# Half blocks of the attention sums and key-value products on 128x64 array tiles, in a kernel of two linear and two sliding-window attention layers

## The chip, the cores and the metric

The kernel runs on one core of a Trainium2 chip. The engines named here are TensorE (PE, with its weight loads as PEld), VectorE (DVE), ScalarE (ACT), GpSimd (POOL) and the queue of SyncE (SP), which issues most transfers. The metric is the device time of one execution in microseconds (us).

## The reference, cut to what matters

Four attention layers of 32 heads, 16 wide, work on one sequence of 2048 tokens with 512 features. Layers one and three are linear attention (A), two and four sliding-window attention (B) with a window of 256 tokens. Each is added to the residual.

```python
def _A_ref(x, wqkv, wo):                       # layers 1 and 3
    q, k, v = ...                              # x @ wqkv, 32 heads of 16
    phi = lambda t: jnp.where(t > 0, t + 1, jnp.exp(t)) + 1e-6
    pq, pk = phi(q), phi(k)
    kv = jnp.einsum("bhsd,bhse->bhde", pk, v)  # summed over all tokens
    z = jnp.einsum("bhsd->bhd", pk)
    num = jnp.einsum("bhqd,bhde->bhqe", pq, kv)
    den = jnp.einsum("bhqd,bhd->bhq", pq, z)[..., None] + 1e-6
    return (num / den) ... @ wo

def _B_ref(x, wqkv, wo):                       # layers 2 and 4
    scores = jnp.einsum("bhqd,bhkd->bhqk", q, k) * (Dh ** -0.5)
    mask = (idx[:, None] - idx[None, :] >= 0) & (idx[:, None] - idx[None, :] < 256)
    p = _softmax(jnp.where(mask, scores, -1e9), axis=-1)
    return jnp.einsum("bhqk,bhkd->bhqd", p, v) ... @ wo

x = A_x
x = x + _A_ref(_layernorm(x), A_wqkv, A_wo)
x = x + _B_ref(_layernorm(x), B_wqkv, B_wo)
x = x + _A_ref(_layernorm(x), A_wqkv, A_wo)
x = x + _B_ref(_layernorm(x), B_wqkv, B_wo)
```

## The kernel before

The tokens are 16 tiles of 128. A linear layer goes over them twice: `a_kv` makes the normalised tile, its transpose `xTa`, phi(k) (`pk`) and v with a column of ones (`vA`), and `kv_mm` (L917) adds each tile's key-value product; once all sixteen are in, `sums` (L1229, the operations fin0 and fin1) masks the result into `kvz`. Then `a_q` and `a_out` make phi(q), the products with `kvz` (L947, the "normalised products") and the output projection. In layer one the sums over all tiles stay in PSUM; in layer three they are gathered in groups and added to `kvacc` on VectorE (L1328).

In a sliding-window layer a token tile is a block of 128 queries that sees six half blocks of 64 keys. Four of them are seen by all 128 queries (the scores `pF`, L1065); the oldest is seen by the first 64 queries only and the newest by the last 64 only (the scores `pH`, L1016). The scores run on row tiles of the array: 32 rows by 128 columns, four heads at a time. ScalarE takes the exponentials (L1086 for pF, L1044 for pH), VectorE multiplies the triangular masks in (L1104, L1052), and TensorE sums the weighted values: L1122 for the half blocks, L1134 for the full ones, into one bank `U` per two quarters of the heads (u0 and u1; the operations u0h and u1h are the half blocks). `vbd` holds the values laid out for two heads and their sum. A half block's matmul is a full 128x128 one. So that the 64 queries which don't see the block get zeros, `pH` has 192 columns per head: 64, then 64 that were set to zero once (`fill_pH`), then 64. The weight operand of the older block is columns 0 to 127, of the newer one columns 64 to 191. The first two token tiles have only the newer half block. The last tile of layer four has its own end, `b_end`, in four pieces (L1170 and L1179).

All operations of the four layers are recorded first, with what they read and write. A written list of numbers, `ORDER`, then gives the order: each word is an operation, a quote mark picks its second engine, and the figures behind a colon pick buffers or PSUM banks. `schedule` takes the words in turn, so each engine's program is the list's order cut down to that engine, and each engine works strictly in its own order. `emit` puts a semaphore wait only where an operation on another engine isn't known to have ended. PSUM has eight banks, and a score set takes two pairs of them. Sets such as `BYPE` say which transposes run on TensorE and not as a transfer, and the `"PE":` numbers beside an operation are the list maker's estimates of length.

A second program, `general`, is recorded beside it for inputs with values that are not finite; it isn't reached here.

Of the kernel before, what the change touches and what calls it, by code (L numbers as in the profile page):

```python
# [8 lines left out]
ACT = mybir.ActivationFunctionType  # L9
ALU = mybir.AluOpType  # L10
AP = bass.AP

P = 128
# [321 lines left out]
205:5.1 148 16 222' 23 272:1 273:13 192 214:6.7.0 215 163 244:7.0.3 245 184:3.1.2 177 216 218 302:2 285 185 286 246 174 303:14 248 250:4.2 251 229:2.2.1 230  # L335
265:7.3 287:3 247 217 249 186 178 266 188 26 219 259:6.3.3 260 274:3.4.0 233 252' 58 187 189 206 288:15 30 199:4.5.2 200 267 261 231 232 280:7.4 262 263 234
203 201 202 275 17 204 235:6.5 236 193 304:4.6.1 237' 207 20 31 264 276 278 277 279 32 33 305 306 307 308 309 289:5.1.2 281 290 208 291 292 293 294 295:6.6
# [6 lines left out]
617:4.3 618 619:0 448:2 405 851:0.2.0 415 852 853 416 631 592 632 417:3 625:7.2.5 406 633:0 626 878:4.0.1 622:6.3 623 648 879 880 649 467:3.10.3 468 627' 854  # L344
# [85 lines left out]
"""  # L430
PHIA = ("1.k","2.q","3.q")
HMD = ("2.a.", "3.a.")
BYPE = {("x1.", t) for t in range(4)} | {("a2.", 15), ("k2.", 15), ("o3.", 0), ("x3.", 0), ("a3.", 15)} | {("o2.",0),("x2.",0)}
VMOVE = {"POOL": 1.03}
KNEAR = {("3.b.", 0)}
LATE = 1
# [944 lines left out]
```

## Time and profile before

| what | us |
|---|---|
| median of three runs | 414.84 |
| lowest and highest | 413.82, 418.99 |
| the profiled execution | 414.87 |
| its span, first to last instruction | 413.6 |
| TensorE busy | 399.4 |
| ScalarE busy | 376.6 |
| VectorE busy | 370.5 |

The granted TensorE clock is 1.00 throughout. A busy share counts the time in which at least one instruction of the engine is under way; matmuls overlap each other, so for TensorE the step from one start to the next says more than the length of one. In the rows quoted later, "x16" counts instructions, `out<-in` names the tiles without their buffer numbers, and the last part tells what the engine waited for.

### The profile page before, as it was taken

How to read it: one execution, taken by the hardware profiler on the slowest of the kernel's cores; microseconds unless marked ns; L12 is line 12 of the kernel's file. 1: busy time of each engine (PE TensorE's matmuls, PEld its weight loads, DVE VectorE, ACT ScalarE, POOL GpSimd, SP SyncE). 2: the span in 40 equal slices, each digit the busy share in tenths (PEclk: the TensorE clock that was granted, in tenths of full speed). 3: DMA queues.
4: the chain of work that ended last, by engine and by line, in shares of the span. 5: the costliest groups of instructions: out<-in, count | busy, mean ns of one | idle time of the engine just before them, and what ended most of it. 6: DMA issues, size and time to landing. Idle time of an engine off the chain costs nothing.

```text
span 413.6 us, 18932 instructions
## 1 busy us (share of the span) xinstructions
PE 399.4 (97%) x8394; PEld 284.3 (69%) x8394; DVE 370.5 (90%) x979; ACT 376.6 (91%) x485; POOL 104.8 (25%) x204
## 2 busy tenths in 40 slices
PE   7999999999999999999999999999999999999998
PEld 2654877776676767777686678676767776867765
DVE  6996799999999999999998999999999999887873
ACT  5998769999999999999999467899999999999996
POOL 2420025162053121411313000260533232311300
DMA  8539224526243235222122102331375453261433
GB/s 259 145 84 217 43 61 80 101 60 99 46 55 57 48 51 69 50 35 61 42 49 55 41 2 40 70 75 32 80 81 76 68 107 34 55 93 30 58 54 92
DMA packets 76808, 29.48 MB, mean 71 GB/s; under 512 B 66352, under 2 KB 74672, under 8 KB 76720
## 3 DMA queue, kind: packets, MB, share of 16 engines
q1 hardware_dynamic: 71424, 22.63, 29.7%
q0 software_dynamic: 4096, 4.46, 6.1%
q8 instruction: 68, 1.11, 1.2%
q10 hardware_dynamic: 1200, 1.11, 0.9%
q14 instruction: 20, 0.16, 0.2%
HBM read 6.29 MB, written 2.10 MB: 20 GB/s over the span
## 4 chain that ended last, share of the span: by engine, by line
PE 50%; ACT 34%; DVE 11%; DMA 3%; issue 1%; SPq 0%; DVEq 0%
ACT pF L1086 24%; PE ps L863 21%; PE ps L875 10%; ACT pH L1044 7%; PE ps L1134 6%; PE ps L1065 5%; PE ps L1122 3%; DVE o L959 2%; DMA w_Av<-in_A_wqkv_dram 2%; PE ps L1016 1%; DVE stats L819 1%; DMA oT<-o 1%; PE ps L921 1%; PE ps L947 1%; DVE pk L890 1%
## 5 line engine op out<-in xcount | busy, mean ns | idle before, releaser
L1086 ACT ACTIVATE pF<-ps 128x1024 bf16<-128x1024 f32 x240 | 229.6, 1083 | 4.4 <-PE ps L1065 2.6
L822 POOL TENSOR_TENSOR rstd<-mv,const 128x1 f32<-128x1 f32 x64 | 37.6, 594 | 211.9 <-DVE mv L820 194.2
L990 POOL DMA_DIRECT2D vbd<-vt x128 | 67.3, 533 | 73.8 <-DVE vt L850 48.6
L1134 PE MATMUL ps<-vbd,pF 128*128 128x34 bf16 x1856 | 62.2, 178 | 1.9 <-issue 1.9
L1044 ACT ACTIVATE pH<-ps 128x1024 bf16<-128x1024 f32 (+1 forms) x64 | 60.3, 1014 | 2.6 <-PE ps L1016 2.3
L1134 PEld LDWEIGHTS ps<-vbd,pF 128*128 128x128 bf16 x1856 | 54.7, 96 | 8.4 <-issue 2.1
L1104 DVE TENSOR_TENSOR pF<-pF,const 128x512 bf16<-128x512 bf16 (+2 forms) x116 | 47.1, 413 | 5.6 <-ACT pF L1086 5.2
L1065 PE MATMUL ps<-qT,kbd 32*128 32x128 bf16 x1920 | 48.7, 217 | 1.9 <-ACT pF L1086 0.6
L884 ACT ACTIVATE E<-ps 128x512 bf16<-128x512 f32 x64 | 38.6, 622 | 10.4 <-PE ps L875 7.8
L819 DVE BATCH_NORM_STATS2 stats<-xres 128x6 f32<-128x512 bf16 x64 | 43.4, 684 | 1.9 <-DMA xres<-in_A_x_dram 1.6
L1052 DVE TENSOR_TENSOR pH<-pH,const 128x1024 bf16<-128x1024 bf16 (+1 forms) x64 | 41.1, 644 | 0.4 <-ACT pH L1044 0.4
L1065 PEld LDWEIGHTS ps<-qT,kbd 32*128 32x128 bf16 x1920 | 28.2, 92 | 17.7 <-ACT pF L1086 7.0
L875 PE MATMUL ps<-xT,w_Bk 128*128 128x128 bf16 x512 | 35.5, 219 | 0.7 <-ACT xT L850 0.3
L875 PE MATMUL ps<-xT,w_Bq 128*128 128x128 bf16 x512 | 35.6, 219 | 0.2 <-ACT pF L1086 0.2
L1122 PEld LDWEIGHTS ps<-vbd,pH 128*128 128x128 bf16 x928 | 29.2, 96 | 9.4 <-issue 3.1
L863 PE MATMUL ps<-w_Av,xTa 128*128 128x512 bf16 (+2 forms) x134 | 33.9, 369 | 1.4 <-DMA w_Av<-in_A_wqkv_dram 1.2
L875 PE MATMUL ps<-xTa,w_Aq 128*128 128x128 bf16 x512 | 34.8, 219 | 0.2 <-DVE pq L888 0.2
L863 PE MATMUL ps<-w_Bv,xT 128*128 128x512 bf16 (+2 forms) x144 | 34.2, 356 | 0.6 <-ACT pF L1086 0.3
L863 PE MATMUL ps<-w_Bo,oT 128*128 128x512 bf16 (+2 forms) x141 | 34.5, 354 | 0.3
L1122 PE MATMUL ps<-vbd,pH 128*128 128x34 bf16 x928 | 32.8, 178 | 1.3 <-DVE pF L1104 0.5
L863 PE MATMUL ps<-w_Ao,oT 128*128 128x512 bf16 (+2 forms) x145 | 33.7, 354 | 0.2
L863 PE MATMUL ps<-w_Ak,xTa 128*128 128x512 bf16 (+1 forms) x131 | 32.7, 374 | 0.6 <-ACT xTa L850 0.5
(98 smaller groups left out, 611.1 us busy)
## 6 DMA issues: line engine op xcount, KB each, us to landing
vbd<-vt POOLq DMA_DIRECT2D x128, 34.0 KB, 2.3
xres<-in_A_x_dram SPq DMA_DIRECT2D x16, 128.0 KB, 5.7
out_dram<-xres SPq DMA_DIRECT2D x15, 128.0 KB, 2.3
oT<-o SPq DMA_TRANSPOSE x60, 2.6
w_Ak<-in_A_wqkv_dram ACTq DMA_DIRECT2D x1, 512.0 KB, 5.5
w_Av<-in_A_wqkv_dram ACTq DMA_DIRECT2D x1, 512.0 KB, 7.6
w_Aq<-in_A_wqkv_dram SPq DMA_DIRECT2D x1, 512.0 KB, 6.6
w_Ao<-in_A_wo_dram SPq DMA_DIRECT2D x1, 512.0 KB, 5.8
```

The costliest lines, as they stand in the source:

```text
L819: s.op(n + ".st", {"DVE": 0.595}, lambda e, en: e.bn_stats(st0, x.h[:]), reads=[x], writes=[st])
L863: i = e.matmul(g.h[:, a:b], xT.h[:, kt, :], w.h[:, kt, a:b], start=(kt == 0), stop=(kt == 3), skip_group_check=True)
L875: i = e.matmul(g.h[:, f * P:(f + 1) * P], w.h[:, kt, f * P:(f + 1) * P], xT.h[:, kt, :], start=(f == 0 and kt == 0), stop=(kt == 3), skip_ ...
L884: s.op(n + ".e", {"ACT": _act_cost(512)}, lambda e, en: e.activation(E.h[:], g.h, ACT.Exp, bias=0.0), reads=[g], writes=[E])
L990: return [e.dma_start(vbd.h[64 * a:64 * a + 64, j, a], vt.h[64 * j:64 * j + 64, a]) for j in range(2)]
L1044: return e.activation(d, c, ACT.Exp, bias=0.0, scale=DH ** -0.5)
L1052: return e.tensor_tensor(v, v, tr, ALU.mult)
L1065: i = e.matmul(ss[r // 2].h[:, r % 2, k * P:k * P + P], kbds[fj[m] // 2].h[32 * r:32 * r + 32, f, fj[m] % 2, :], qT.h[32 * r:32 * r + 32, ...
L1086: s.op("e%d%d" % (u, g), {"ACT": _act_cost(1024)}, lambda e, en, S=ss[g], pb=pb, g=g: e.activation(pb.h[:, 2 * g:2 * g + 2, :], S.h, ACT.E ...
L1104: return e.tensor_tensor(v, v, tr, ALU.mult)
L1122: i = e.matmul(U.h[:, c:c + 34], pH.h[:, 4 * r + f, 64 * a:64 * a + P], vbds[j // 2].h[:, j % 2, :, 4 * f + r, :], start=first[0], stop=Tr ...
L1134: i = e.matmul(U.h[:, c:c + 34], pFs[at[f, m][0]].h[:, r, at[f, m][1] * P:at[f, m][1] * P + P], vbds[fj[m] // 2].h[:, fj[m] % 2, :, 4 * f ...
```

## The change

Every half block is now its own 64 queries wide. `pH` shrinks from 192 to 128 columns per head and needs no zeros. The matmul of the older half block uses the left 64 columns of the array and writes PSUM partitions 0 to 63, that of the newer one the right 64 columns and partitions 64 to 127; `tile_position` says so, and the two stand one behind the other. The key-value product of a quarter of the heads is cut in the same way: two matmuls with 64 columns of `pk` and 68 columns of `vA` where there was one of 128 by 136. Only a matching half of each former product was used, so the sums need one PSUM bank in place of two, `kvacc` half the size, and `sums` spreads them over the mask. In layer one the products are issued for four tiles at a time (`KV1`) and no longer tile by tile. The half-block sums no longer name the masked `pF` among what they read, and where there is no older half block they come behind the full blocks. One more of the first transposes is a transfer. `PHIP` is empty and changes nothing. `ORDER` is a new list.

```diff
 ORDER = """
-8 0 9 39 1 2 10 63:7 69 5 6 4 7 3 41 42 40 11 70 71 72 73:0 68 43 44 45 74:6.0 64 46 47 48 86 18 35 37 87 75 76:7.0.0 88 12 13 77 27 14 15 24 89:1 28 22
...
-BYPE = {("x1.", t) for t in range(4)} | {("a2.", 15), ("k2.", 15), ("o3.", 0), ("x3.", 0), ("a3.", 15)} | {("o2.",0),("x2.",0)}
+BYPE = {("x1.", t) for t in range(3)} | {("a2.", 15), ("k2.", 15), ("o3.", 0), ("x3.", 0), ("a3.", 15)} | {("o2.",0),("x2.",0)}
-LATE = 1
+KV1 = [4, 4, 4, 4]
+KV2 = [4, 4, 4, 2, 1, 1]
+PHIP = set()
...
-            self.r_pH = self.preset("pH", 3, [P, 16, 192], self.fill_pH())
+            self.r_pH = self.ring("pH", 3, [P, 16, P])
...
-    def kv_mm(self, pairs, dst, new, start):
+    def kv_mm(self, pairs, g, new, start):
         def mm(e, en):
-            d = dst()
             for n, (pk, vA) in enumerate(pairs):
                 for f in range(4):
-                    i = e.matmul(d[f // 2][:, (f % 2) * 136:(f % 2) * 136 + 136], pk.h[:, f * P:(f + 1) * P],
-                                 vA.h[:, 8 * f:8 * f + 8, :], start=(start and n == 0 and f % 2 == 0), stop=True,
-                                 skip_group_check=True)
+                    for c in range(2):
+                        i = e.matmul(g.h[64 * c:64 * c + 64, f * 68:f * 68 + 68], pk.h[:, f * P + 64 * c:f * P + 64 * c + 64],
+                                     vA.h[:, 8 * f + 4 * c:8 * f + 4 * c + 4, :], start=(start and n == 0 and f == 0), stop=True,
+                                     skip_group_check=True, tile_position=(0, 64 * c))
             return i
...
                         for a, j in pcs:
                             c = ((f % 2) * 4 + r) * 34
-                            i = e.matmul(U.h[:, c:c + 34], pH.h[:, 4 * r + f, 64 * a:64 * a + P], vbds[j // 2].h[:, j % 2, :, 4 * f + r, :],
-                                         start=first[0], stop=True, skip_group_check=True)
-                            first[0] = False
+                            i = e.matmul(U.h[64 * a:64 * a + 64, c:c + 34], pH.h[:, 4 * r + f, 64 * a:64 * a + 64], vbds[j // 2].h[:, j % 2, :, 4 * f + r, :],
+                                         start=(len(pcs) == 2 and f == 2 * g and r == 0), stop=True, skip_group_check=True, tile_position=(0, 64 * a))
...
-                        i = e.matmul(U.h[:, r * 34:r * 34 + 34], pH.h[:, 4 * r + f, 64 * a:64 * a + P], vbds[j // 2].h[:, j % 2, :, 4 * f + r, :],
-                                     start=(r == 0 and j == pcs[0][1]), stop=True, skip_group_check=True)
+                        i = e.matmul(U.h[64 * a:64 * a + 64, r * 34:r * 34 + 34], pH.h[:, 4 * r + f, 64 * a:64 * a + 64], vbds[j // 2].h[:, j % 2, :, 4 * f + r, :],
+                                     start=(r == 0), stop=True, skip_group_check=True, tile_position=(0, 64 * a))
...
-            self.kv_mm([(pk, vA)], lambda: (kvS.h[:, 0, :], kvS.h[:, 1, :]), [kvS] if t == 0 else [], t == 0)
+            group.append((pk, vA))
+            if len(group) == KV1[done]:
+                self.kv_mm(group, kvS, done == 0, done == 0)
+                group, done = [], done + 1
...
                 def acc(e, en, g2=g2, ngrp=ngrp):
-                    for hf in range(2):
-                        d = self.kvacc[:, 2 * hf:2 * hf + 2, :].rearrange("p f c -> p (f c)")
-                        i = e.tensor_copy(d, g2[hf].h[:, 0:272]) if ngrp == 0 else e.tensor_tensor(d, g2[hf].h[:, 0:272], d, ALU.add)
-                    return i
+                    d = self.kvacc[:].rearrange("p f c -> p (f c)")
+                    return e.tensor_copy(d, g2.h[:, 0:272]) if ngrp == 0 else e.tensor_tensor(d, g2.h[:, 0:272], d, ALU.add)
```

What the new list does to TensorE's order shows at three places. The first is the end of layer one's key-value phase; before, the products (L921) of single tiles follow the last value projections (`w_Av` with `xTa`), then a query projection (L875) and the first normalised products (L947):

```order
L863 MATMUL ps<-w_Av_135,xTa_63 128x512 x4
L863 MATMUL ps<-w_Av_135,xTa_62 128x512 x4
L921 MATMUL ps<-vA_122,pk_75 128x136 x4
L921 MATMUL ps<-vA_122,pk_70 128x136 x4
L921 MATMUL ps<-vA_122,pk_68 128x136 x4
L921 MATMUL ps<-vA_122,pk_71 128x136 x4
L921 MATMUL ps<-vA_122,pk_72 128x136 x4
L921 MATMUL ps<-vA_122,pk_69 128x136 x4
L921 MATMUL ps<-vA_122,pk_74 128x136 x4
L875 MATMUL ps<-xTa_53,w_Aq_136 128x128 x16
L947 MATMUL ps<-kvz_94,pq_77 128x136 x2
```

After, with L855 for the projections, L913 for the products, L867 and L935 for what follows:

```order
L855 MATMUL ps<-w_Av_137,xTa_63 128x448
L855 MATMUL ps<-w_Av_137,xTa_63 128x64
L913 MATMUL ps<-vA_122,pk_68 64x68 x8
L913 MATMUL ps<-vA_122,pk_70 64x68 x8
L913 MATMUL ps<-vA_122,pk_69 64x68 x8
L913 MATMUL ps<-vA_122,pk_73 64x68 x8
L913 MATMUL ps<-vA_122,pk_71 64x68 x8
L913 MATMUL ps<-vA_122,pk_74 64x68 x8
L913 MATMUL ps<-vA_122,pk_72 64x68 x8
L913 MATMUL ps<-vA_122,pk_75 64x68 x8
L867 MATMUL ps<-xTa_52,w_Aq_138 128x128 x16
L935 MATMUL ps<-kvz_94,pq_77 128x136 x2
```

The last two groups of four tiles stand together, and the last of them holds the tile whose value projection (`xTa_63`) comes just ahead.

The second place is in layer four, the half sums of one token tile between two score sets; before:

```order
L1065 MATMUL ps<-qT_100,kbd_125 128x128 x4
L1134 MATMUL ps<-vbd_132,pF_103 128x34 x16
L1122 MATMUL ps<-vbd_132,pH_133 128x34 x16
L875 MATMUL ps<-xT_46,w_Bk_138 128x128 x8
L1065 MATMUL ps<-qT_99,kbd_128 128x128 x4
```

After (L1052 scores, L1123 full-block sums, L1107 half-block sums):

```order
L1052 MATMUL ps<-qT_100,kbd_125 128x128 x4
L1123 MATMUL ps<-vbd_132,pF_103 128x34 x16
L1107 MATMUL ps<-vbd_132,pH_134 64x34 x16
L1123 MATMUL ps<-vbd_132,pF_107 128x34 x16
L1052 MATMUL ps<-qT_99,kbd_128 128x128 x4
```

The half sums keep their place among full-array matmuls, and are now of another tile shape than both neighbours.

The third place, a little later, shows half sums right behind a score set; before:

```order
L1065 MATMUL ps<-qT_101,kbd_126 128x128 x4
L863 MATMUL ps<-w_Bv_140,xT_45 128x512 x2
L1122 MATMUL ps<-vbd_132,pH_133 128x34 x16
L1134 MATMUL ps<-vbd_132,pF_107 128x34 x16
L1065 MATMUL ps<-qT_101,kbd_124 128x128 x4
```

After:

```order
L1052 MATMUL ps<-qT_101,kbd_126 128x128 x4
L1107 MATMUL ps<-vbd_132,pH_135 64x34 x16
L1123 MATMUL ps<-vbd_132,pF_105 128x34 x16
L1123 MATMUL ps<-vbd_132,pF_106 128x34 x16
L1052 MATMUL ps<-qT_98,kbd_125 128x128 x4
```

Here the three tile shapes follow each other: row tiles, column tiles, full array.

More of the change, by code (lines that the diff above doesn't have):

```diff
@@ L484, in run @@
             self.r_dn = self.ring("dn", 4, [P, 32], F32)
-            self.kvacc = self.tiles("kvacc", 1, [P, 4, 136], F32)[0]
+            self.kvacc = self.tiles("kvacc", 1, [P, 4, 68], F32)[0]
             self.r_vA = self.preset("vA", 8, [P, 32, 17], self.fill_vA())
@@ L1121, in pvH, with half, pvF @@
                             c = ((f % 2) * 4 + r) * 34
[L1122 to L1128 removed]
+                            i = e.matmul(U.h[64 * a:64 * a + 64, c:c + 34], pH.h[:, 4 * r + f, 64 * a:64 * a + 64], vbds[j // 2].h[:, j % 2, :, 4 * f + r, :],
+                                         start=(len(pcs) == 2 and f == 2 * g and r == 0), stop=True, skip_group_check=True, tile_position=(0, 64 * a))
+                return i
+            side = len(pcs) == 2
+            def half(new):
+                s.op("u%dh" % g, {"PE": 0.27 if side else 0.25}, pvH, reads=[pH] + [vbds[j // 2] for _, j in pcs], writes=[U], new=new, mode="c", kind="sum")
+            if side:
+                half([U])
             for f in (2 * g, 2 * g + 1):
[L1130 removed]
+                def pvF(e, en, f=f, g=g, U=U, side=side):
                     for r in range(4):
@@ L1134, in pvF @@
                             i = e.matmul(U.h[:, c:c + 34], pFs[at[f, m][0]].h[:, r, at[f, m][1] * P:at[f, m][1] * P + P], vbds[fj[m] // 2].h[:, fj[m] % 2, :, 4 * f + r, :],
-                                         start=False, stop=True, skip_group_check=True)
+                                         start=(not side and f == 2 * g and r == 0 and m == m0), stop=True, skip_group_check=True)
                     return i
-                s.op("u%d%d" % (g, f % 2), {"PE": 0.0252 * 4 * (4 - m0)}, pvF, reads=use(f) + [vbds[j // 2] for j in fj[m0:]], writes=[U], kind="sum")
+                s.op("u%d%d" % (g, f % 2), {"PE": 0.0252 * 4 * (4 - m0)}, pvF, reads=use(f) + [vbds[j // 2] for j in fj[m0:]], writes=[U],
+                     new=[U] if not side and f == 2 * g else [], kind="sum")
+            if not side:
+                half([])
             dn = self.r_dn.buf()
@@ L1306, in graph @@
         s.at = ("1.", base)
-        self.sums(lambda hf: kvS.h[:, hf, 0:272], kvz)
+        self.sums(lambda: kvS.h[:, 0:272], kvz)
         b1 = base + 0.1
@@ L1313, in graph @@
         ngrp = 0
-        groups = [4, 4, 4, 2, 1, 1]
+        groups = KV2
         for t in range(T):
@@ L1336, in graph @@
         s.at = ("2.", b2)
-        self.sums(lambda hf: self.kvacc[:, 2 * hf:2 * hf + 2, :].rearrange("p f c -> p (f c)"), kvz2)
+        self.sums(lambda: self.kvacc[:].rearrange("p f c -> p (f c)"), kvz2)
         self.segment("3.", b2, xTs2, kvz2, True)
```

192 lines of the change are left out of this document (89 added, 103 removed), and 75 rows, old and new, of the table ORDER.

## The prediction

> **What bounds the kernel now.** I read the page's busy shares first, then the busy time stage by stage, then what ScalarE waits for, then single stretches of TensorE's timeline.
>
> ```profile
> span 413.6 us, 18932 instructions
> PE 399.4 (97%) x8394; PEld 284.3 (69%) x8394; DVE 370.5 (90%) x979; ACT 376.6 (91%) x485; POOL 104.8 (25%) x204
> PE 50%; ACT 34%; DVE 11%; DMA 3%; issue 1%; SPq 0%; DVEq 0%
> ```
>
> Two engines are nearly full. The third line, the chain that ended last, is half TensorE and a third ScalarE. An average hides which of them binds where, so here is the same by stage. The first figure is the length, then the busy time of PE, PEld, DVE, ACT, POOL.
>
> ```profile
> 2.00:45.00 43.00, 41.30 (x296) 22.95 (x295) 33.83 (x113) 34.51 (x61) 9.05 (x16) 1.00 0.64 172
> 45.00:80.00 35.00, 34.01 (x590) 25.89 (x588) 34.08 (x95) 29.32 (x47) 8.67 (x16) 1.00 0.38 65
> 80.00:220.00 140.00, 137.18 (x3196) 99.07 (x3194) 130.70 (x332) 136.06 (x163) 38.97 (x72) 1.00 0.34 59
> 220.00:263.00 43.00, 42.19 (x655) 30.54 (x651) 40.11 (x111) 30.69 (x52) 5.70 (x11) 1.00 0.18 34
> 263.00:408.00 145.00, 140.19 (x3614) 103.24 (x3615) 128.58 (x322) 142.94 (x162) 41.61 (x78) 1.00 0.41 66
> 408.00:413.60 5.60, 3.70 (x57) 2.37 (x56) 2.25 (x8) 1.87 (x5) 0.00 (x0) 1.00 0.29 94
> ```
>
> From 2 to 80 us and from 220 to 263 us TensorE is full and ScalarE has gaps: 8.5, 5.7 and 12.3 us of them. From 263 to 408 us ScalarE is the full one: 142.94 of 145. What it waits for in that stretch (total, times, longest):
>
> ```profile
> ACT pF L1086 <- PE ps L1065: 0.8, 3, 0.5
> ACT pF L1086 <- PE ps L1072: 0.5, 1, 0.5
> ACT pH L1044 <- PE ps L1016: 0.2, 1, 0.2
> ```
>
> So 1.5 us at most of the last 145 us hang on TensorE. Between 80 and 220 us both are full.
>
> **What TensorE's work costs.** A "mode" is the tile shape of the array: full 128x128, or row tiles (32x128, the scores). The change adds column tiles (128x64). The trace holds no column tile, so its price has to come from neighbouring rows.
>
> ```profile
> 41.77 1.82 PE L921 MATMUL ps<-vA,pk 128*128 128x136 bf16 x28
> 43.42 1.06 PE L875 MATMUL ps<-xTa,w_Aq 128*128 128x128 bf16 x16
> 44.32 0.40 PE L947 MATMUL ps<-kvz,pq 128*128 128x136 bf16 x4
> ...
> 153.58 0.56 PE L1122 MATMUL ps<-vbd,pH 128*128 128x34 bf16 x16
> 154.08 0.40 PE L1065 MATMUL ps<-qT,kbd 32*128 32x128 bf16 x16
> 154.41 0.62 PE L875 MATMUL ps<-xT,w_Bq 128*128 128x128 bf16 x8
> ...
> 386.06 0.96 PE L1134 MATMUL ps<-vbd,pF 128*128 128x34 bf16 x32
> 387.14 0.41 PE L1016 MATMUL ps<-qT,kbd 32*128 32x64 bf16 x32
> 387.48 0.61 PE L863 MATMUL ps<-w_Bo,oT 128*128 128x512 bf16 x2
> ```
>
> The first figure is the start, the second the length. Matmuls overlap, so I take start to start.
> - Key-value products: (43.42 - 41.77) / 28 = 59 ns each, 0.236 us for the four of a token tile.
> - A 128-column full-array matmul: (44.32 - 43.42) / 16 = 56 ns.
> - Attention sums with 34 columns:
>
> ```profile
> L1134 PE MATMUL ps<-vbd,pF 128*128 128x34 bf16 x1856 | 62.2, 178 | 1.9 <-issue 1.9
> L1122 PE MATMUL ps<-vbd,pH 128*128 128x34 bf16 x928 | 32.8, 178 | 1.3 <-DVE pF L1104 0.5 <-ACT kt L850 0.2 <-ACT qT L850 0.2
> ```
>
> One lasts 178 ns; 32 in a row last 0.96 us, so the step is (0.96 - 0.178) / 31 = 25.2 ns, and sixteen cost 0.404 us.
> - A turn from one mode to another: sixteen sums ahead of row tiles take 154.08 - 153.58 = 0.50 us, 0.10 more than 0.404. The row-tile scores then take 0.33: four sets of four tiles stream 128 columns each, 4 x 56 = 0.224, so 0.106 is left for the turn back. I count **0.10 us a turn**.
> - A set of four row tiles with 64 columns: (387.48 - 387.14 - 0.10) / 8 = 30 ns.
>
> **The change, part by part.**
>
> *Half-block sums.* Of the 928 matmuls on L1122, 864 are 54 full groups of sixteen (27 token tiles, two groups each); 64 belong to the eight one-sided groups of the first two tiles of each layer. A full group becomes eight pairs. Bounds for a pair with 34 columns: 25 ns if it costs what one matmul costs now, 50 ns if nothing overlaps. I take **30 ns**, the row-tile set of 64 columns, the only row in which tiles share the array with so few columns. Per group 8 x 30 = 0.240 against 0.404: 54 x -0.164 = **-8.9 us** (range -11 to 0). One-sided groups have no partner: 8 x 8 x 5 ns = +0.3 us. The last tile's four groups of eight (L1170) go from 0.202 to 0.120: -0.3 us.
>
> *Key-value products.* Four matmuls become four pairs with 68 columns, between 30 ns (64) and 56 ns (128): 32 ns. 32 token tiles x (0.128 - 0.236) = **-3.5 us**.
>
> *Turns.* Counted over the whole order of TensorE, mode changes go from 306 to 381. 75 x 0.10 = **+7.5 us**. By stage: six more before the first normalised products, 28 up to the last key-value group of layer three, 36 to the last tile, five in the tail. The order shows why: a half group used to stand among other full-array sums, and is now an island between row tiles and full tiles, or between two full groups, which costs two.
>
> *Smaller edits.* Transposes on TensorE go from ten to nine: 4 x 56 ns = -0.2 us at the start. The tenth becomes a DMA on SP's queue, which sends the later tiles' transposes behind it; TensorE has the three tiles before it to work on meanwhile. The accumulation on VectorE halves:
>
> ```profile
> L1328 DVE TENSOR_TENSOR kvacc<-ps,kvacc 128x272 f32<-128x272 f32 x10 | 3.9, 433 | 0.0
> L705 ACT ACTIVATE pH<-const 128x1536 f32<-128x1536 f32 x1 | 1.5, 1506 | 0.0
> L850 ACT ACTIVATE qT<-ps 128x512 bf16<-128x512 f32 x12 | 7.6, 633 | 0.8 <-PE ps L875 0.8
> L850 DVE CAST qT<-ps 128x512 bf16<-128x512 f32 x20 | 13.7, 683 | 1.7 <-PE ps L875 1.6
> ```
>
> With its two copies it is twelve of about 0.43, now six: -2.6 us of VectorE, which TensorE hides between 180 and 247 us. The fill of pH goes (1.5 us of ScalarE at 14 us, in its slack), and ScalarE gives VectorE three 512-column copies on balance (0.63 each), all before the last stage. In that stage ScalarE's exponentials and copies stay the same in number, but for one of 128 columns at the very end. If VectorE's slack were gone, the three copies would cost 3 x 0.68 = 2 us. The half sums no longer wait for a masked pF; the L1122 row above shows 0.5 us of that wait, which I leave at nothing.
>
> *A new wait.* The last key-value group of the first phase needs four tiles at once, and stands right behind the last value projection. [...] After it the masking of the sums on VectorE (0.79 us in the first line below) is still covered by sixteen query matmuls (0.90):
>
> ```profile
> 43.63 0.79 DVE L1232 TENSOR_TENSOR kvz<-ps,const 128x272 bf16<-128x272 f32 x2 [1.96 <-PE ps L921]
> ```
>
> *Sum by stage*, on the path and off it:
> - To 44 us, TensorE bound: products -1.7, turns +0.6, transpose -0.2, wait +0.4: **-0.9**, all on the path.
> - 44 to about 250 us: 28 groups -4.6, four one-sided +0.2, products -1.7, turns +2.8: -3.3 of TensorE. ScalarE fills two thirds of this stretch as fully, so I carry half: **-1.7** (0 to -3.3).
> - The layer-four stage: 26 groups -4.3, one-sided +0.1, turns +3.6: -0.6, off the path, since ScalarE sets it: **0**.
> - Tail: sums -0.3, turns +0.5: **+0.2**.
>
> Together -2.4 us. The profiled execution took 414.87 us (span 413.6 and 1.3 around it), next to the median of 414.84, so I forecast **412.5 us**: within 2% (8.3 us), about what a measurement of this kernel can tell from no change.
>
> **The weight loads.** A load of 128 columns lasts 96 ns here, yet matmuls follow every 25 ns, so loads overlap each other about fourfold:
>
> ```profile
> L1122 PEld LDWEIGHTS ps<-vbd,pH 128*128 128x128 bf16 x928 | 29.2, 96 | 9.4 <-issue 3.1 <-DVE mv L820 0.4 <-DVE qT L850 0.4
> ```
>
> [...]
>
> **Rivals.**
> - *The halves do not overlap* (50 ns a pair, no gain in sums or products). Then only turns and the wait are left: +0.8 to 44 us, +2.8 after, up to +3.6 in the last stage, where TensorE has 4.8 us free, +0.5 in the tail: +4.1 to +7.7, about **420**. For it: 34 columns already step at 25 ns. Against: row tiles of 64 columns manage four in 30 ns.
> - *Each load is exposed*: half of 96 ns, one after the other. A full group costs 16 x 48 = 0.768, +0.364; the products of a tile 8 x 48 = 0.384, +0.148. To 44 us +3.2; then 28 x 0.364 + 2.4 + 2.8 = +15.4; last stage 9.5 + 3.6 less 4.8 free = +8.3; tail +1.2: **443**. Against: loads overlap in every mode that the trace has.
> - *Scores come late to the full ScalarE* (the slower side). TensorE works strictly in order, and an island of 0.24 and two turns, 0.44 us, now stands ahead of a score set in many places. If each of the 26 in the last stage shows as an idle gap of ScalarE, that is +11.4 from there: **424**. It decides once the islands use up the lead that TensorE has in PSUM, of eight banks four for a set. For it: 142.94 of 145 leaves nothing. Against: 1.5 us of such waits before, and TensorE's load is no higher than before.
> - *The new order packs better*: pairs at 25 ns (-1.0 to 44 us, -4.8 to 250 us, all on the path), and a quarter of ScalarE's 12.3 idle us between 220 and 263 filled, -3: **406**. One bank in place of two for the products speaks for it, nothing else.
>
> **How the numbers follow.** Forecast, with the case that nothing passes through, 410.5 to 415: 0.48. No overlap (419 to 422.5): 0.17. Scores late: 0.17. Better packed: 0.13. Loads exposed: 0.05. The 2% bounds are 406.5 and 423.1. Faster takes nearly all of "better packed", 0.12; slower takes the exposed loads and most of the late scores, 0.18; within 2% is 0.70. The range 405 to 421 leaves out the two slow cases' upper ends, 0.2.
>
> **What would show it.** In the profile after: the sixteen half sums start to start near 0.24 us beside other column work, and near 0.34 ahead of another mode; products 0.13 a tile; ScalarE still full in the last stage; the last stage as long as before; the first normalised products about 1 us earlier. The forecast is wrong if a pair costs over 50 ns, if a turn with column tiles costs far from 0.10, or if ScalarE's waits for scores grow past 5 us.

## The result

The changed kernel takes 411.86 us (median of 19 runs, 409.51 to 415.72) against 414.84 (19 runs of the kernel before). The ratio is 0.9928, with a 95% interval of 0.9902 to 0.9954: about 3 us faster, under 2% and clear of no change. The forecast was 412.5. Executions of one kernel differ in the mean granted TensorE clock (the kernel before, on one chip: medians of 414.3, 415.2 and 416.8 us at 1.00, 0.996 and 0.992), so differences near 1 us are also read from profiles at 1.00.

### The profile page after: what moved, and what is told of

Read it like the earlier page. It is cut to its first block, busy times and chain, and to the rows that moved or that the text cites. A ratio compares the mean times of both kernels' runs of the same rounds, so it can differ in the third digit from the quotient of the medians.

```text
span 410.6 us, 19193 instructions
## 1 busy us (share of the span) xinstructions
PE 395.3 (96%) x8539; PEld 277.5 (68%) x8539; DVE 370.6 (90%) x979; ACT 373.2 (91%) x481; POOL 107.4 (26%) x204
## 3 DMA queue, kind: packets, MB, share of 16 engines
q1 hardware_dynamic: 71968, 22.76, 29.5%
## 4 chain that ended last, share of the span: by engine, by line
ACT 45%; PE 30%; DVE 19%; DMA 3%; issue 1%; SPq 1%; POOL 0%; DVEq 0%; POOLq 0%
ACT pF L1073 34%; PE ps L855 11%; ACT pH L1031 8%; PE ps L867 7%; PE ps L1123 4%; DVE stats L811 3%; PE ps L1052 3%; DMA xres<-in_A_x_dram 2%; DVE o L947 2%; DMA xTa<-xn 2%; PE ps L1107 2%; PE ps L1004 1%; DVE xres L890 1%; DVE xn L817 1%; DVE E L877 1%
## 5 line engine op out<-in xcount | busy, mean ns | idle before, releaser
L814 POOL TENSOR_TENSOR rstd<-mv,const 128x1 f32<-128x1 f32 x64 | 39.5, 620 | 216.8 <-DVE mv L812 216.5
L1123 PE MATMUL ps<-vbd,pF 128*128 128x34 bf16 x1856 | 60.6, 178 | 0.3
L1123 PEld LDWEIGHTS ps<-vbd,pF 128*128 128x128 bf16 x1856 | 54.0, 96 | 7.5 <-issue 0.6
L1052 PE MATMUL ps<-qT,kbd 32*128 32x128 bf16 x1920 | 49.1, 217 | 2.9 <-ACT pF L1073 0.8
L1052 PEld LDWEIGHTS ps<-qT,kbd 32*128 32x128 bf16 x1920 | 28.5, 92 | 19.9 <-ACT pF L1073 8.0
L867 PE MATMUL ps<-xT,w_Bq 128*128 128x128 bf16 x512 | 36.2, 219 | 0.2
L867 PE MATMUL ps<-xT,w_Bk 128*128 128x128 bf16 x512 | 35.6, 219 | 0.4
L855 PE MATMUL ps<-w_Ao,oT 128*128 128x512 bf16 (+2 forms) x145 | 34.4, 355 | 0.9 <-ACT pF L1073 0.6
L855 PE MATMUL ps<-w_Ak,xTa 128*128 128x512 bf16 (+1 forms) x133 | 33.2, 371 | 1.9 <-DMA xTa<-xn 1.3
L855 PE MATMUL ps<-w_Bv,xT 128*128 128x512 bf16 (+2 forms) x148 | 35.1, 351 | 0.0
L855 PE MATMUL ps<-w_Bo,oT 128*128 128x512 bf16 (+2 forms) x149 | 34.3, 344 | 0.5 <-DVE mv L812 0.2
L867 PE MATMUL ps<-xTa,w_Aq 128*128 128x128 bf16 x512 | 33.9, 219 | 0.0
L855 PE MATMUL ps<-w_Av,xTa 128*128 128x512 bf16 (+2 forms) x141 | 32.6, 360 | 1.3 <-DMA w_Av<-in_A_wqkv_dram 1.3
L867 PEld LDWEIGHTS ps<-xTa,w_Aq 128*128 128x128 bf16 x512 | 29.9, 98 | 3.9 <-ACT pF L1073 0.7
L867 PEld LDWEIGHTS ps<-xT,w_Bq 128*128 128x128 bf16 x512 | 29.7, 98 | 4.1 <-issue 0.9
```

The source lines that it names most:

```text
L814: s.op(n + ".rs", {"POOL": 0.53}, lambda e, en: e.tensor_tensor(a_rs, v, self.half.h[:], ALU.pow), reads=[mv, self.half], writes=[rs])
L855: i = e.matmul(g.h[:, a:b], xT.h[:, kt, :], w.h[:, kt, a:b], start=(kt == 0), stop=(kt == 3), skip_group_check=True)
L867: i = e.matmul(g.h[:, f * P:(f + 1) * P], w.h[:, kt, f * P:(f + 1) * P], xT.h[:, kt, :], start=(f == 0 and kt == 0), stop=(kt == 3), skip_ ...
L1052: i = e.matmul(ss[r // 2].h[:, r % 2, k * P:k * P + P], kbds[fj[m] // 2].h[32 * r:32 * r + 32, f, fj[m] % 2, :], qT.h[32 * r:32 * r + 32, ...
L1123: i = e.matmul(U.h[:, c:c + 34], pFs[at[f, m][0]].h[:, r, at[f, m][1] * P:at[f, m][1] * P + P], vbds[fj[m] // 2].h[:, fj[m] % 2, :, 4 * f ...
```

## The profile after

The profiled execution took 411.86 us too. The page's first and fourth part:

```profile
span 410.6 us, 19193 instructions
PE 395.3 (96%) x8539; PEld 277.5 (68%) x8539; DVE 370.6 (90%) x979; ACT 373.2 (91%) x481; POOL 107.4 (26%) x204
ACT 45%; PE 30%; DVE 19%; DMA 3%; issue 1%; SPq 1%; POOL 0%; DVEq 0%; POOLq 0%
```

TensorE is busy 4.1 us less than before, VectorE the same, ScalarE 3.4 us less. In the chain that ended last ScalarE and TensorE have changed places. The same by stage (length, then PE, PEld, DVE, ACT, POOL):

```profile
2.00:45.00 43.00, 39.70 (x361) 21.17 (x360) 35.06 (x119) 31.10 (x59) 9.25 (x16) 1.00 0.76 188
45.00:80.00 35.00, 34.45 (x595) 26.29 (x592) 34.68 (x96) 29.32 (x45) 9.99 (x18) 1.00 0.39 67
80.00:220.00 140.00, 136.58 (x3287) 96.99 (x3285) 132.49 (x336) 136.34 (x162) 42.32 (x75) 1.00 0.32 55
220.00:263.00 43.00, 42.73 (x678) 31.00 (x677) 39.28 (x108) 32.86 (x55) 5.16 (x10) 1.00 0.21 36
263.00:408.00 145.00, 140.74 (x3626) 101.69 (x3623) 127.60 (x318) 141.91 (x162) 39.77 (x74) 1.00 0.38 66
```

In the first stage TensorE now idles 3.3 us, before 1.7. Between 220 and 263 us ScalarE works 2.2 us more than before in the same 43 us, so the work around it has moved together.

Fixed windows can't show where 3 us went, so the next cut is by events. The first row of each kernel goes from 80 us to the end of layer two's last exponential, the second from there to the start of layer four's first, the third to the end of layer four's last. Before:

```profile
80.00:228.96 148.96, 145.94 (x3385) 104.81 (x3383) 138.24 (x352) 144.88 (x174) 42.27 (x78) 1.00 0.33 57
228.96:261.65 32.69, 32.17 (x446) 24.27 (x443) 31.28 (x86) 20.52 (x39) 2.19 (x4) 1.00 0.16 30
261.65:408.87 147.22, 142.31 (x3653) 104.39 (x3652) 130.03 (x326) 145.16 (x165) 41.83 (x78) 1.00 0.41 67
```

After:

```profile
80.00:229.17 149.17, 145.75 (x3510) 104.00 (x3508) 140.11 (x356) 145.24 (x174) 42.88 (x76) 1.00 0.32 54
229.17:258.52 29.35, 29.08 (x384) 20.51 (x383) 27.25 (x77) 19.87 (x37) 2.19 (x4) 1.00 0.18 29
258.52:405.50 146.98, 142.72 (x3661) 103.58 (x3659) 130.82 (x326) 145.12 (x165) 42.17 (x78) 1.00 0.39 68
```

**The gain stands in one place.** Layer two ends where it did (229.17 against 228.96), layer four is as long as it was (146.98 against 147.22), and the stretch between them, in which TensorE is full and ScalarE a third empty, shrinks from 32.69 to 29.35 us. TensorE has 3.1 us less to do in it. Part of what is gone are query projections of layer three, which now stand ahead of layer two's end; before and after, in that stretch:

```profile
L875 PE MATMUL ps<-xTa,w_Aq 128*128 128x128 bf16 x176 | 11.9, 219 | 0.0
```

```profile
L867 PE MATMUL ps<-xTa,w_Aq 128*128 128x128 bf16 x144 | 9.4, 219 | 0.0
```

**What the new tiles cost.** TensorE's timeline in layer four and at the end of the first phase, after:

```profile
324.96 0.40 PE L1052 MATMUL ps<-qT,kbd 32*128 32x128 bf16 x16
325.29 0.43 PE L1107 MATMUL ps<-vbd,pH 128*64 128x34 bf16 x16
325.65 0.98 PE L1123 MATMUL ps<-vbd,pF 128*128 128x34 bf16 x32
...
41.80 0.70 PE L913 MATMUL ps<-vA,pk 128*64 128x68 bf16 x32
42.66 0.70 PE L913 MATMUL ps<-vA,pk 128*64 128x68 bf16 x32 [0.15 <-DVE vA L842]
43.29 1.07 PE L867 MATMUL ps<-xTa,w_Aq 128*128 128x128 bf16 x16
44.19 0.75 PE L935 MATMUL ps<-kvz,pq 128*128 128x136 bf16 x10
```

```profile
L1107 PE MATMUL ps<-vbd,pH 128*64 128x34 bf16 x928 | 25.1, 186 | 0.9 <-ACT vt L842 0.2 <-ACT kt L842 0.2 <-ACT pF L1073 0.2
L913 PE MATMUL ps<-vA,pk 128*64 128x68 bf16 x256 | 5.5, 196 | 0.2 <-DVE vA L842 0.2
```

Sixteen half sums are eight pairs: (0.43 - 0.186) / 7 = 35 ns a pair, 0.28 us a group. They take 0.36 us start to start ahead of full tiles, so the turn back is 0.08. The row tiles ahead of them take 0.33, as before, so the turn to column tiles costs the 0.10 that a turn cost then. Four token tiles of products: (0.70 - 0.196) / 15 = 34 ns a pair, 0.13 us a tile. The last key-value group shows an idle time of 0.15 us in its row; from start to start the 16 pairs ahead of it take 0.86 us (41.80 to 42.66) in place of 0.54, so the new wait costs TensorE 0.32.

**What came in unasked.** TensorE idles in the first phase for a transposed tile, and SP's queue shows why. TensorE and SP, after:

```profile
34.79 3.63 PE L855 MATMUL ps<-w_Ak,xTa 128*128 128x512 bf16 x16 [1.27 <-DMA xTa<-xn]
```

```profile
20.53 7.12 SPq L825 DMA_TRANSPOSE xTa<-xn  x5
27.69 0.58 SPq L771 DMA_DIRECT2D w_Ao<-in_A_wo_dram  x1
28.32 5.81 SPq L825 DMA_TRANSPOSE xTa<-xn  x3
```

Before, SP issued the load of `w_Ao` (512 KB) nearly last, with one transposition behind it; now three stand behind it:

```profile
19.12 12.33 SPq L833 DMA_TRANSPOSE xTa<-xn  x8
31.50 0.58 SPq L779 DMA_DIRECT2D w_Ao<-in_A_wo_dram  x1
32.12 1.19 SPq L833 DMA_TRANSPOSE xTa<-xn  x1
```

## The experiments

One profiled execution carries its own start: how long TensorE waits for the first weights differs from one to the next (1.2 us for `w_Av` before; 1.3 for `w_Av` and 0.6 for `w_Ak` after). So the table splits eight profiled executions, all at a mean granted clock of 1.00, at the start of the first normalised products.

| kernel | ratio to before [95%] | first normalised products, us | from there to the end of the span | layer two's last exponential to layer four's first | layer four's exponentials |
|---|---|---|---|---|---|
| before | 1 | 44.3 | 369.3 | 32.7 | 147.2 |
| changed | 0.9928 [0.9902, 0.9954] | 44.2 | 366.4 | 29.4 | 147.0 |
| sums on the full array | 0.9948 [0.9921, 0.9975] | 44.4 | 367.7 | 29.5 | 147.0 |
| products on the full array | 0.9909 [0.9877, 0.9941] | 42.9 | 367.2 | 29.7 | 147.2 |
| both on the full array | 0.9963 [0.9937, 0.9988] | 45.2 | 368.0 | 29.9 | 147.4 |
| old order, sums on column tiles | 1.0010 [0.9991, 1.0028] | 44.2 | 368.9 | 32.8 | 147.1 |
| halves in turn, not in pairs | 0.9971 [0.9947, 0.9994] | 42.9 | 367.9 | 29.6 | 147.3 |
| layer four's half sums twice | 1.0064 [1.0040, 1.0087] | 44.8 | 371.8 | 29.4 | 153.1 |

### Undoing the tiles, keeping the order

The half sums go back to 128 columns (`pH` is 192 wide again, with zeros in the middle, filled once):

```diff
-i = e.matmul(U.h[64 * a:64 * a + 64, c:c + 34], pH.h[:, 4 * r + f, 64 * a:64 * a + 64], vbds[j // 2].h[:, j % 2, :, 4 * f + r, :],
-             start=(len(pcs) == 2 and f == 2 * g and r == 0), stop=True, skip_group_check=True, tile_position=(0, 64 * a))
+i = e.matmul(U.h[:, c:c + 34], pH.h[:, 4 * r + f, 64 * a:64 * a + P], vbds[j // 2].h[:, j % 2, :, 4 * f + r, :],
+             start=(len(pcs) == 2 and f == 2 * g and r == 0 and a == 0), stop=True, skip_group_check=True)
```

> The changed kernel with its half-block sums (864 of 928 matmuls and the last tile's 32) back on the full array, in the same order of all engines; the products stay on column tiles, the result stays the reference's. In the changed kernel's trace a pair of half sums steps at 35 ns, so a group costs 0.28 us against 0.404: undoing adds 54 x 0.124 = +6.7 us of TensorE, and takes away 65 turns (381 to 316) x 0.095 = -6.2. Theory A (the sums nearly pay for their own turns; products and TensorE time freed ahead of layer four make the gain): 411.9 +- 1.2. Rival (the sums carry the gain): back to 414 or more. Rival (the new order carries the gain): 411.9 as well.

Measured: 413.69 us, 0.9948 [0.9921, 0.9975], 0.8 us above the changed kernel by the ratios and 1.3 us by the stretch behind the first normalised products. That lies between the theory's 411.9 and the rival's 414. The intervals overlap, so the size is open; both readings say that the turns saved pay for most of what the pairs bring, and that the pairs bring more.

The key-value products go back to four matmuls a tile:

```diff
-for c in range(2):
-    i = e.matmul(g.h[64 * c:64 * c + 64, f * 68:f * 68 + 68], pk.h[:, f * P + 64 * c:f * P + 64 * c + 64],
-                 vA.h[:, 8 * f + 4 * c:8 * f + 4 * c + 4, :], ..., tile_position=(0, 64 * c))
+i = e.matmul(g.h[:, f * 124:f * 124 + 136], pk.h[:, f * P:(f + 1) * P], vA.h[:, 8 * f:8 * f + 8, :], ...)
```

> The changed kernel with its key-value products on the full array again, four matmuls of 136 columns per token tile in place of eight of 68; sums stay on column tiles, same order. The four results overlap in the one bank, so the output is not the reference's; instruction count, sizes and waits are those of a full product. TensorE: 32 x (0.236 - 0.142) = +3.0 us, six turns fewer -0.6. All of it lies ahead of layer four. Theory A: +1.5 to +2.4 us, 413.4 to 414.3. Rival (order carries the gain): 411.9.

Measured: 411.55 us, 0.9909 [0.9877, 0.9941]. The theory that the products carry the gain falls: within the intervals nothing is lost without them. In the trace the wait for the transposed tile is gone instead. From 30 to 43 us, TensorE busy 11.57 us in the changed kernel and 12.95 here:

```profile
30.00:43.00 13.00, 11.57 (x133) 5.76 (x132) 9.16 (x29) 9.32 (x18) 0.00 (x0) 1.00 1.05 231
```

```profile
30.00:43.00 13.00, 12.95 (x110) 7.99 (x109) 9.43 (x32) 8.81 (x18) 0.00 (x0) 1.00 0.76 219
```

One reading is that the quicker products of the first phase only let TensorE reach a late tile sooner; but that wait differs between profiles of one order (more on it below), so it is not shown. Behind the first normalised products this kernel is 0.8 us longer than the changed one; the products of layer three, 16 x 0.10 us dearer here, would explain it.

Both edits together leave the new order with the smaller edits:

> Both undone, the new order alone: every matmul on the full array or on row tiles, 306 turns as before the change; output as with full products. TensorE: +6.7 + 3.0 - 7.1 = +2.6 us over the changed kernel. Theory A: 413.5 to 415, the time before the change. Rival (the new order carries the gain): 411.9 or less.

Measured: 414.35 us, 0.9963 [0.9937, 0.9988], near theory A. It is 1.5 us under the kernel before by the ratio, 1.3 us by the stretch behind the first normalised products, and 0.8 us where only executions at a granted clock of 1.00 are compared. Its cut by the same events as above:

```profile
80.00:231.06 151.06, 144.58 (x3457) 107.61 (x3491) 141.39 (x359) 146.36 (x175) 42.87 (x76) 1.00 0.33 54
231.06:260.91 29.85, 29.47 (x347) 21.27 (x351) 27.37 (x77) 19.86 (x37) 2.19 (x4) 1.00 0.18 29
```

The order shortens the stretch between the layers to 29.85 by itself. What it moves ahead of layer two's end then lengthens layer two: that ends at 231.06, 1.9 us later than in the changed kernel.

### The tiles in the old order

The kernel before, with its half sums on column tiles and nothing moved; the key-value products stay as they were:

```diff
-i = e.matmul(U.h[:, c:c + 34], pH.h[:, 4 * r + f, 64 * a:64 * a + P], ...)
+i = e.matmul(U.h[64 * a:64 * a + 64, c:c + 34], pH.h[:, 4 * r + f, 128 * a:128 * a + 64], ..., tile_position=(0, 64 * a))
```

> The kernel before with its two-sided half sums on column tiles, in its own old order; products, one-sided sums and everything else as before, the result stays the reference's. TensorE: 52 or 54 groups x -0.124 = -6.7 us, and mode changes go from 306 to 400, 94 x 0.095 = +8.9: +2.2 us. Theory (without the new order the turns eat the gain): 0 to +2 us over the time before. Rival (the tile shape gains in any order): -2 to -3.

Measured: 414.61 us, 1.0010 [0.9991, 1.0028], as expected. By the sum 400 turns against 306 eat what the pairs save, and the stretch between the layers stays at 32.8. Neither half of the change makes the 3 us: sums alone nothing, order alone about 1 to 1.5.

### Do the two halves overlap?

The sixteen matmuls of a group run left, left, ... right, right instead of left, right, left, right:

```diff
-for f in (2 * g, 2 * g + 1):
-    for r in range(4):
-        for a, j in pcs:
+for a, j in pcs:
+    for f in (2 * g, 2 * g + 1):
+        for r in range(4):
```

> The changed kernel with the sixteen half sums of a group in another order: all eight on the left 64 columns, then all eight on the right. Same instructions, tiles, waits and turns; neighbours no longer lie on different tiles. Theory (the 35 ns of a pair come from two tiles at work at the same time): each of the sixteen then takes about a pair's time, 31 to 35 ns, a group 0.50 to 0.56, +0.25 x 54 = +13 us of TensorE, about half of it in layer four where 4.3 are free: 418 to 422. Rival (a 64-column matmul simply costs 17.5 ns, paired or not): no change, 411.9.

Measured: 412.99 us, 0.9971 [0.9947, 0.9994]. The overlap is real: with the 186 ns of one from the second row, the group in the first row (layer four, the first ahead of a normalised product) steps at (0.58 - 0.186) / 15 = 26 ns a matmul, against 35 ns for two in a pair.

```profile
321.25 0.58 PE L1107 MATMUL ps<-vbd,pH 128*64 128x34 bf16 x16
...
L1107 PE MATMUL ps<-vbd,pH 128*64 128x34 bf16 x928 | 32.2, 186 | 0.7 <-ACT vt L842 0.2 <-ACT kt L842 0.2
```

A lone half sum is thus no dearer than a full-array one (25 ns), so a group costs 16 x 0.026 = 0.42 us in place of 0.28. That is 54 x 0.14 = 7.6 us of TensorE, of which 1.8 us showed by the ratios and 1.5 by the stretch behind the first normalised products: the size that was expected fell, the overlap did not.

### How much of TensorE's time passes through

The half sums of 28 groups ahead of layer three's key-value end (layer two) run twice, the second run starting the bank anew, so that the sums stay the same; then the same is done in layer four (`"3.a."`):

```diff
-def pvH(e, en, g=g, U=U):
-    for f in (2 * g, 2 * g + 1):
-        for r in range(4):
+def pvH(e, en, g=g, U=U, again=2 if len(pcs) == 2 and s.at[0] == "2.a." else 1):
+    for f, r in [(f, r) for _ in range(again) for f in (2 * g, 2 * g + 1) for r in range(4)]:
```

> The changed kernel with the 28 two-sided groups of half sums of layer two issued twice (the second pass writes the same bank anew, the result stays the reference's). That is 28 x 0.28 = +7.8 us of TensorE between 60 and 229 us. Theory (TensorE's work before layer four sets the time nearly one for one, since what it can't do there of layer three's projections is left for the stretch without exponentials): +5.5 to +8, 417.5 to 420. Prediction's half share: +3.9, 416. Rival (ScalarE, 136 of 140 us busy there, sets it): 0 to +2.

Measured: 418.30 us, 1.0088 [1.0056, 1.0120]. The busy time of the half sums (25.1 us in the changed kernel) is 32.0 here, so TensorE had 6.9 us more to do, and by the ratios the kernel became 6.6 us longer, give or take 1.7 by the intervals: layer two passes TensorE's time on nearly one for one.

> The same in layer four: 26 groups twice, +7.3 us of TensorE between 263 and 403 us, where ScalarE is busy 141.9 of 145 us and TensorE 140.7. Theory (ScalarE sets layer four, TensorE has some 4.3 us free): 0 to +3.5, 412 to 415.5. Rival (TensorE sets it as well): +7, 419.

Measured: 417.59 us, 1.0064 [1.0040, 1.0087], 5.6 us longer (give or take 1.4) for 6.7 us of extra work (half sums 31.8 us in place of 25.1); layer four's exponentials take 153.1 in place of 147.0. The share passed on is not told apart from layer two's. The theory that ScalarE alone sets layer four falls. ScalarE's groups from 258 us on, in the changed kernel and in this one:

```profile
L1073 ACT ACTIVATE pF<-ps 128x1024 bf16<-128x1024 f32 x120 | 114.0, 1126 | 0.9 <-PE ps L1052 0.7
L1031 ACT ACTIVATE pH<-ps 128x1024 bf16<-128x1024 f32 (+1 forms) x32 | 30.5, 1045 | 1.2 <-PE ps L1004 1.1
```

```profile
L1073 ACT ACTIVATE pF<-ps 128x1024 bf16<-128x1024 f32 x120 | 114.4, 1034 | 3.6 <-PE ps L1052 1.7 <-PE ps L1059 1.2
L1031 ACT ACTIVATE pH<-ps 128x1024 bf16<-128x1024 f32 (+1 forms) x32 | 29.3, 972 | 1.9 <-PE ps L1004 1.7
```

The idle time ahead of exponentials grows from 2.1 to 5.5 us. The mean of one full-block exponential falls (1126 to 1034 ns) while the busy time does not: 120 of them add up to 135.1 us in 114.0 us of busy time in the changed kernel and to 124.1 in 114.4 here, so the time in which two run at once falls from 21.1 to 9.7 us. A late score set costs the wait here, and the overlap with it. TensorE is busy 144.5 of those 153.1 us and is not full either, which points to the place of the longer sums in its order and not to their total.

### The late tile

In the changed kernel the load of `w_Ao` goes behind the three transposing transfers on SP's queue, one word of the list:

```diff
-183 231:0 232:12 57 197:3.0 136 166
+183 231:0 232:12 197:3.0 136 166
...
-254:6.3 205:5.2.1 223 289:15 58 59
+254:6.3 205:5.2.1 223 289:15 57 58 59
```

> The changed kernel with one word of the order moved: SP issues the load of the output weights of layer one behind the last three transposes of the first phase and no longer ahead of them. In the changed kernel TensorE stands 1.27 us at 33.5 us for such a transpose (xTa), three of which take 5.8 us there. Theory (the load of 512 KB delays the transposes): the wait goes, -0.5 to -1.2 us, 411. Rival (the transposes are late for another reason, their tiles or other loads): no change.

Measured: 410.29 us, 0.9872 [0.9829, 0.9915]. Both kernels once more, side by side on one chip:

> The changed kernel once more, as the mark for the three below on one chip. Expected: 411.9 us, 0.993 of the kernel before (0.990 to 0.996). It holds the 1.27 us stall of TensorE at 35 us, ahead of the key projection that waits for a transposed tile.

> The changed kernel with one transfer moved: the load of w_Ao stands one place later on SP's queue, behind the three transposing transfers instead of ahead of them. Theory (the stall at 35 us lies on the path and is carried to the end): about 1.3 us under the changed kernel on the same chip, 410.5, 0.990 of the kernel before. Rival (what is saved at 35 us is lost again at a later wait, layer two being held by ScalarE too): within 0.4 us of the changed kernel.

Measured: 411.91 us, 0.992 [0.989, 0.995], for the changed kernel and 410.67, 0.9897 [0.9866, 0.9928], with the later load: 1.24 us apart, with overlapping intervals and the same sign both times. At a granted clock of 1.00 each of the five executions with the later load (410.6 to 411.0) lies below each of the five without (411.1 to 412.9). SP's queue then, the stretch from 30 to 43 us, and TensorE's key projections to 44 us, which wait for weights only:

```profile
20.50 13.70 SPq L825 DMA_TRANSPOSE xTa<-xn  x8
34.25 0.58 SPq L771 DMA_DIRECT2D w_Ao<-in_A_wo_dram  x1
```

```profile
30.00:43.00 13.00, 12.85 (x159) 7.03 (x158) 10.00 (x34) 9.62 (x19) 0.00 (x0) 1.00 0.74 207
```

```profile
L855 PE MATMUL ps<-w_Ak,xTa 128*128 128x512 bf16 (+1 forms) x65 | 15.8, 376 | 0.5 <-DMA w_Ak<-in_A_wqkv_dram 0.5
```

SP is through with the last transposition no earlier (28.32 + 5.81 = 34.1 us in the changed kernel, 34.2 here), so it isn't SP's time that the tile missed. With the load ahead, its 512 KB move in the same stretch as the last transposing transfers: issued at 27.69 us, they land 5.0 us later. The transposing transfers of the changed kernel between 24 and 40 us take 3.0 us from issue to landing (the median of six), and 2.6 here; from 30 to 43 us the DMA share, the last but one figure of the row, is 1.05 in the changed kernel and 0.74 here. That the load's packets held the tile back is the reading that fits, and it is not shown: with products on the full array the load stands ahead too, and the share is 0.76 and there is no wait; with the halves in turn it is 1.05 and the wait 0.2 us. The wait is no constant either: in the nine profiles with the load ahead it is 0 to 1.8 us, in the three with it behind there is none. This is the fastest kernel of the case.

### Four copies to VectorE

Four copies out of PSUM in layer four get the quote mark that gives them to VectorE:

```diff
-1956:0 1982 2015 2010:0
+1956':0 1982' 2015' 2010':0
```

> The changed kernel with four copies out of PSUM of layer four given from ScalarE to VectorE, nothing else moved. ScalarE has 2.5 us less to do in layer four (4 x 0.63), VectorE about 2.7 us more of its 16 us of slack there, TensorE the same. Theory A (ScalarE alone sets the last stage): 2 to 2.5 us under the changed kernel, 409.5. Theory B (TensorE is as full there, as the doubled half sums of layer four let suppose, which cost 5.6 of their 7.0 us): 0 to 0.8 us under it, 411.5.

Measured: 417.50 us, 1.0058 [1.0031, 1.0085]: 5.6 us slower than the changed kernel on that chip, outside both theories. In the profile nearly all of it is one place. ScalarE and VectorE there:

```profile
324.60 5.61 ACT L1073 ACTIVATE pF<-ps 128x1024 bf16<-128x1024 f32 x6 [0.51 <-PE ps L1052]
334.26 1.02 ACT L1073 ACTIVATE pF<-ps 128x1024 bf16<-128x1024 f32 x1 [4.06 <-PE ps L1052]
```

```profile
329.32 0.69 DVE L842 CAST qT<-ps 128x512 bf16<-128x512 f32 x1 [1.24 <-PE ps L867]
331.84 0.69 DVE L842 CAST kt<-ps 128x512 bf16<-128x512 f32 x1 [1.06 <-PE ps L867]
332.90 0.69 DVE L947 TENSOR_TENSOR o<-ps,dn 128x512 bf16<-128x512 f32 x1
```

And TensorE:

```profile
330.74 1.07 PE L867 MATMUL ps<-xT,w_Bk 128*128 128x128 bf16 x16 [1.46 <-DVE o L1138]
331.64 0.40 PE L935 MATMUL ps<-kvz,pq 128*128 128x136 bf16 x4
333.73 0.49 PE L1052 MATMUL ps<-qT,kbd 32*128 32x128 bf16 x16 [1.69 <-DVE o L947]
```

VectorE's copy of `qT` waits for the query projection, and behind it on VectorE stands the division (L1138) that frees the bank TensorE needs for the key projection; the copy of `kt` then waits for that projection, and behind it stands the division (L947) that frees the bank of the next scores. Two waits each way, 4.06 us without a score for ScalarE. VectorE had 16 us to spare in the stage, and none in its order. The run is therefore no test of whether ScalarE sets the stage.

Right behind the two waits TensorE's granted clock falls, and ScalarE waits for scores once more:

```profile
334.00:337.00 3.00, 3.00 (x65) 1.54 (x53) 2.11 (x6) 1.94 (x2) 0.00 (x0) 0.50 0.23 49
337.19 1.94 ACT L1031 ACTIVATE pH<-ps 128x1024 bf16<-128x1024 f32 x2 [0.98 <-PE ps L1004]
```

The clock, the last but two figure of the first row, is 0.50 for some 3.3 us, and the wait behind it 0.98 us. All twelve executions have a mean clock of 0.988 to 0.996, five of the six of the changed kernel on that chip 1.00. So the 5.6 us hold the ring of waits and a slower clock. Whether the waits bring the clock down is not shown: behind the 1.27 us that TensorE stood idle in the changed kernel it stayed at 1.00.

> Both edits together: the later load of w_Ao and the four copies on VectorE. If both gains are real and apart, their sum: by theory A of the copies 408 us, by theory B 410, 0.984 to 0.989 of the kernel before. If the first gain is lost again later, as much as the copies alone give.

Measured: 415.38 us, 1.0001 [0.9977, 1.0025]: 4.7 us above the kernel with the later load alone, nearly the same loss, at the same two waits. Two of its twelve executions have a mean clock of 1.00 and take 414.3 and 414.8 us, 3.9 above the 410.6 of the later load alone at that clock: so much is the waits, and the rest of the 5.6 goes with the clock.

## Why the prediction was right, and where it was not

The time was forecast 0.6 us too high, out of steps that were not all of the right size.

- **Pairs overlap: right, price 5 ns low.** 30 ns was taken, 35 ns measured. A group costs 0.28 instead of 0.24 us, so 54 groups bring 54 x (0.404 - 0.28) = 6.7 us instead of 8.9. The nearest row (row tiles of 64 columns) was the right one to lean on, and the rivals "no overlap" and "each load exposed" fall with it.
- **The weight loads.** Row by row, the narrow load is the longer one:

```profile
L1123 PEld LDWEIGHTS ps<-vbd,pF 128*128 128x128 bf16 x1856 | 54.0, 96 | 7.5 <-issue 0.6
L1107 PEld LDWEIGHTS ps<-vbd,pH 128*64 128x64 bf16 x928 | 20.0, 112 | 7.5 <-issue 3.1 <-ACT pq L879 0.6 <-ACT pF L1073 0.6
```

  112 ns for 64 columns against 96 for 128. A pair, with two such loads, steps at 35 ns all the same: loads overlap in this mode too.
- **Products: right.** 32 ns a pair forecast, 34 measured.
- **Turns: right.** 0.10 forecast, 0.08 to 0.10 measured. That 94 more turns cancel the half sums' gain in the old order shows their weight.
- **To 44 us, -0.9: wrong in the trace, -0.1 (-0.4 in the second profile of the changed kernel).** The step that failed is "TensorE has the three tiles before it to work on meanwhile": the work was there, the transfer came later still, and TensorE stood 1.27 us. The prediction left out the place of the `w_Ao` load on SP's queue: with the load behind the transposes the wait is gone and the first normalised products start at 43.2 us. The kernel with full-array products had no such wait and lost nothing by the medians. No run shows the 0.4 us that the sum has for the wait of the last group, an estimate of the author's; the changed kernel showed 0.32 us, and the rows of the kernel with the four copies show handovers of 0.03 us from TensorE to VectorE (331.81 to 331.84) and 0.14 back (333.59 to 333.73).
- **44 to 250 us, -1.7: the size was off.** It assumed that half of TensorE's gain passes through because ScalarE is as full. From the first normalised products to layer three's last key-value group the timelines show 198.7 us (44.19 to 242.91) where there were 201.8 (44.32 to 246.13): -3.1, at the far end of the range given (-2.8 in the second profile). Doubling the half sums of layer two puts the share at 6.6 of 6.9 us. Behind the share stands the order, which the prediction counted only for its turns: it moves work of layer three out of the stretch that TensorE alone fills into layer two, and the cheaper sums make room for it there. The prediction had a rival for that ("the new order packs better", a quarter of ScalarE's 12.3 idle us), with 0.13 and on top of pairs at 25 ns; its -3 between the two layers came (32.69 to 29.35), the pairs did not.
- **Layer four, 0: right in number (-0.2), not in its reason.** ScalarE's waits for scores stayed small (1.1 us for pH and pF from 263 to 408 us), so "scores late to ScalarE" did not come. But TensorE is no spare engine there: with 6.7 us more on it, 6.1 us show, as late scores. So the mechanism of the rival "scores come late" is there; the half sums of the change, 0.28 us a group, did not set it off, and those of 0.53 us did. The change left layer four alone, as far as the trace tells, because TensorE's load there hardly changed (142.72 us busy against 142.31).
- **Tail, +0.2: right.** From the last exponential to the end 5.05 us, before 4.71.

So two errors met: 0.8 us of the first phase that did not come, and 1.4 us behind it that came on top. That the total lies so near the forecast is in part luck.

What stays open: why 7.6 us of extra TensorE work as unpaired halves cost 1.8 us, while 6.9 or 6.7 us put into one layer cost nearly all. In layer four the unpaired halves lengthen each group by 0.14 us instead of 0.26 and cost 0.3 us in all; a lead of TensorE over ScalarE that takes up the one and not the other would explain it, and was not measured. Which part of the new order packs the work better isn't shown either: the query projections above are one piece of it.

## What to carry to other kernels

Price a new tile shape by the nearest shape that the trace has (30 ns a pair from row tiles of 64 columns, 35 measured), and count its turns over the whole order: here 94 turns were worth as much as pairing the half sums. Where TensorE and ScalarE were both 97 to 98% busy (136.58 and 136.34 of 140 us, 140.74 and 141.91 of 145), extra work on TensorE showed in the time, 6.6 of 6.9 us in layer two and 5.6 of 6.7 in layer four; that is found by giving an engine more work, not by the higher share. And move work between engines or queues only after reading what stands behind it there: one load ahead of three transposing transfers cost 1.2 us by the medians (411.91 against 410.67), and four copies on an engine with 16 us to spare cost 5.6, of which about 4 were the waits that they closed to a ring.

## What the runs showed of the hardware

- A half sum on 64 columns of the array steps at 26 ns when its neighbours use the same columns (halves in turn), one on 128 columns at 25 ns (kernel before); two on different columns step at 35 ns together (changed kernel).
- A weight load of 64 columns on a column tile lasts 112 ns, one of 128 on the full array 96 ns (changed kernel), and a pair of half sums steps at 35 ns all the same.
- A turn between column tiles and another tile shape cost 0.08 to 0.10 us in the changed kernel, one between row tiles and the full array 0.10 in the kernel before.
- In the kernel with the four copies the granted TensorE clock fell to 0.50 for some 3.3 us behind two waits of 1.46 and 1.69 us, and all but two of the 24 executions with these copies have a mean clock below 1.00.
- Three transposing transfers issued behind a 512 KB load took SP 5.81 us in the changed kernel, and TensorE waited 1.27 us for a tile (0.8 in the second profile of the same kernel); with the products on the full array they took 4.97 us and it waited for none, and with the load behind them it didn't wait for any.
